# A turn two steps behind its powers, eight buffers for stored exponentials, and a product with one temporary less, in a fused state-space and gated-layer kernel

## The chip, the cores and the metric

One core of one Trainium2 chip. The metric is device microseconds of one execution. Most executions of a kernel agree within 0.3%, so each experiment has five rounds against the kernel before on the same chip (the main comparison has more), and every ratio a 95% interval.

TensorE does the matmuls (PE in the profile, PEld for its weight loads), VectorE is DVE, ScalarE is ACT, GpSimd is POOL, and SyncE (SP) issues most DMAs.

## The reference

Forward and backward of a sum of two branches over a layer-normed input `xn` of 2048 x 576 in bf16: a gated layer (576 to 4608 and back), and a diagonal state-space convolution with 128 states a channel.

```python
K = einsum("dn,dnl,dn->dl", C, exp(dt * A * l), dt * B).real     # kernel rows, 576 x 2048
y = irfft(rfft(K, 2L) * rfft(u, 2L))[:L] + u * Dskip             # convolution
out = x + y(xn) + (relu(xn @ W_gate) * (xn @ W_up)) @ W_down
# asked for: out, and the gradients of all inputs but one
```

## The kernel before

The kernel is written as two Python generators that a driver interleaves. One emits the gated layer (TensorE's main load: lines 235, 261, 288, 325, 341), the other the convolution. A tile scheduler then decides, at build time, the order of the instructions on each engine, and allots buffers from pools. That order is fixed when the kernel runs. An engine that waits for its next instruction does not take a later one that is ready: below, VectorE stands 5.36 us in front of an exponential, while behind it waits a copy (`ps_s_2070`) whose matmul was done at 131.4 us.

The convolution's second stage handles four channels a step, 144 steps in all:

```python
# driver
g.psum_mm = pool("psum_mm", 5, space=PSUM)     # gated layer
g.psum_s4 = pool("psum_s4", 3, space=PSUM)     # convolution: self.ps() takes one of these
...
# p2: for each group of 32 channels, for each half of 16
    ...  # set-up of 16 channels on VectorE and ScalarE, lines 817 to 842; makes A, B, X, XC
    for dd in range(x0, x0 + SX, DG):                       # four channels a step
        V = uvp.tile(...);  Y = yop.tile(...)               # Y: 3 buffers, V: 1
        v.tensor_tensor(vw(Y), Ap(0), Bp(1), op=ALU.mult)   # line 853  "powers"
        v.tensor_tensor(vw(V), Ap(1), Bp(0), op=ALU.mult)   # line 854
        v.tensor_tensor(Y[:], Y[:], V[:], op=ALU.add)       # line 855
        pend.append((Y, XC, X, ...))
        if len(turned) > 0:
            self.sums(turned.pop(0), uvp)
        if len(pend) > 1:                                   # one step behind
            yield from self.turn(pend.pop(0), ytp, turned)

def turn(...):      # "kernel rows and turned powers"
    psk = self.ps() # 8 matmuls of Y with XC, line 879: kernel rows; a copy to Kst
    pst = self.ps() # 8 transposes of Y, line 889; a copy to YT, on ScalarE mostly
def sums(...):
    psg = self.ps() # 8 matmuls of YT, line 902
    for vi, r0 in enumerate((1, 0)):
        nc.vector.tensor_tensor(pr[:, vi], X[...], psg[...], op=ALU.mult)   # line 906, reads PSUM
    nc.vector.tensor_reduce(...)                                            # line 907
```

Two more places are touched. The stored decay exponentials, 36 tiles of 320 KB, are made early and written to DRAM:

```python
exp_ = self.pool(c, "par_ex", 5)
def ex_step(i):
    ex = exp_.tile(shp, F32, name="exs")
    v.tensor_tensor(ex[:], pw..., self.ev..., op=ALU.mult)      # line 568
    nc.scalar.activation(ex[:], ex[:], ACT.Exp)                 # line 569
    nc.sync.dma_start(self.ex_dram[:, i], ex[:])                # line 570
```

And the complex product of two spectra takes seven VectorE instructions, with temporaries `t` and `w` of two rows each.

## Time and profile before

| | before |
|---|---|
| time, median of the first 6 runs | 1805.5 us (1801.1 to 1808.5) |
| TensorE busy / VectorE busy | 95% / 73% of 1800.3 us |
| TensorE idle in 300 to 1500 us (powers, turns, sums) | about 40 us |

The page of the kernel before opens with the busy time, its share of the span and the number of instructions of each engine:

```profile
span 1800.3 us, 41947 instructions
## 1 busy us (share of the span) xinstructions
PE 1711.7 (95%) x16303; PEld 1185.1 (66%) x16449; DVE 1310.8 (73%) x2867; ACT 1187.4 (66%) x2736; POOL 204.3 (11%) x246
```

TensorE bounds the kernel, so time can be won only from its idle 88.6 us and from stretches at a reduced clock. (146 matmul records are missing in this trace, so a few us of that idle time are not real.)

The view of one tile, here the powers `Y` in the kernel before, lists what idle time of an engine just before an instruction that touches the tile was ended by (us in total, number of waits). TensorE (PE) and its weight loads (PEld) are in it, so that one stall of TensorE is mostly counted twice, and VectorE where it writes `Y`:

```profile
its engine sat idle before it (us, times) until:
  DVE V L906: 25.8, 32
  PE ps_s_4647 L889: 15.0, 1
  issue: 8.4, 9
```

Readers of `Y`, which are the turn's matmuls, wait until VectorE's products in `sums` (line 906, which write `V`) are through. Those products have nothing to do with this `Y`. What they free is a PSUM bank: the turn needs one of three, and the sums of the step before hold one until line 906 has read it. The worst case, as the timeline of TensorE and then of VectorE shows it (start, duration, instruction, count, and in brackets the idle time before it with what ended it):

```profile
574.51 0.35 PE L902 MATMUL ps_s_9294<-dkc,YT 128*128 128x32 bf16 x8
574.72 1.26 PE L288 MATMUL ps_mm<-wf,T 128*128 128x288 bf16 x9
575.81 0.29 PE L633 MATMUL ps_s_9322<-pr_z,IM 128*128 128x288 bf16 x1
575.94 0.35 PE L879 MATMUL ps_s_9325<-XC,Y 128*128 128x16 bf16 x8
578.62 0.62 PE L889 MATMUL ps_s_9335<-ident_bf,Y 128*128 128x128 bf16 x8 [2.33 <-DVE V L906]
579.08 2.15 PE L288 MATMUL ps_mm<-wf,T 128*128 128x288 bf16 x9
```

```profile
574.56 0.69 DVE L855 TENSOR_TENSOR Y<-Y,V 128x1024 bf16<-128x1024 bf16 x1
575.16 0.69 DVE L834 TENSOR_TENSOR X<-W,ex 128x512 f32<-128x512 f32 x1
575.88 0.69 DVE L841 TENSOR_TENSOR W<-pw,X 128x512 f32<-128x512 f32 x1
576.49 0.68 DVE L840 TENSOR_TENSOR xa<-pw,X 128x512 f32<-128x512 f32 x1
577.21 0.69 DVE L842 TENSOR_TENSOR XC<-xa,W 128x512 bf16<-128x512 f32 x1
577.82 0.74 DVE L906 TENSOR_TENSOR V<-X,ps_s_9294 128x256 f32<-128x256 f32 x2
```

The sums' matmuls are done at 574.9. Their bank, `ps_s_9294`, is read only at 577.8, because a power and four instructions of the next channels' set-up stand in front on VectorE. Two more banks have gone out meanwhile (9322, 9325), so the transposes (9335) get the first one back and wait 2.33 us. Nine matmuls of line 288 then take 2.15 us where nine took 1.26 before: the trace has the granted clock at 0.50 for 3.41 us from 579.29 us. The Trainium skill ("TensorE: Matmul & The Clock Gate", Part 1) describes a gate that halves TensorE's clock after an idle window.

The other reading that the prediction rests on is about the exponentials. VectorE waits for a free buffer, and a PSUM copy stands behind the waiting instruction (timeline of VectorE, then of TensorE, kernel before):

```profile
123.81 1.55 DVE L568 TENSOR_TENSOR exs<-pw,ev 128x640 f32<-128x640 f32 x2
127.08 0.46 DVE L61 CAST fA_1905<-ps_s_1933 128x288 bf16<-128x288 f32 x1 [1.72 <-PE ps_s_1933 L609]
127.58 0.46 DVE L61 CAST fA_1937<-ps_s_1941 128x288 bf16<-128x288 f32 x1
133.40 0.83 DVE L568 TENSOR_TENSOR exs<-pw,ev 128x640 f32<-128x640 f32 x1 [5.36 <-DMA ex_dram<-exs]
134.14 0.60 DVE L61 CAST obd<-ps_mm 128x432 bf16<-128x432 f32 x1
134.65 0.45 DVE L61 CAST fA_2069<-ps_s_2070 128x288 bf16<-128x288 f32 x1
...
```

```profile
135.16 0.28 PE L609 MATMUL ps_s_2099<-sig,Sx 128*128 128x288 bf16 x1 [2.66 <-DVE fA_2069 L61]
135.28 1.85 PE L325 MATMUL ps_mm<-rows,hN 128*128 128x144 bf16 x16
```

The table of stretches for 130 to 140 us (busy us and instructions of each engine, then the granted clock, the DMA share and GB/s) shows the clock at 0.83 and the DMA engines nearly full:

```profile
130.00:140.00 10.00, 7.34 (x74) 6.59 (x73) 3.05 (x7) 5.28 (x14) 0.00 (x0) 0.83 0.99 348
```

### The profile page before, as it was taken

To read this page: it belongs to the slowest core of one execution; us is meant where nothing else is said; L and a number is where in the kernel's file an instruction comes from. 1 tells how busy PE (TensorE), PEld (TensorE's weight loads), DVE (VectorE), ACT (ScalarE), POOL (GpSimd) and SP (SyncE) were. 2 spreads that over 40 slices of the span, in tenths; PEclk is the share of its full clock that TensorE was granted. 3 is DMA by queue.
4 is the path that set the end of the run, shared out by engine and by line. 5 is a ranking of instruction groups with operands and counts; after the bars stand their busy time and mean duration, and the time that the engine had idled before them with its cause. 6 is when DMAs were issued, how large, how long until landed. Compare 5 with 4: busy or idle time off the path is not lost. (4 is left out here: it accounts for less than half of the span.)

```text
span 1800.3 us, 41947 instructions
## 1 busy us (share of the span) xinstructions
PE 1711.7 (95%) x16303; PEld 1185.1 (66%) x16449; DVE 1310.8 (73%) x2867; ACT 1187.4 (66%) x2736; POOL 204.3 (11%) x246
## 2 busy tenths in 40 slices
PE   7989999999999999999999999999999998999998
PEld 4665557667566666766756766766676675576776
DVE  7575885677888788668777889889888863872551
ACT  5875874696577578568468657748847745864651
POOL 0200011012022012012102101101101100110000
PEclk9999999999999999999999999999999999999999
DMA  8798999678567566766857856756666578994873
GB/s 294 265 331 298 327 248 284 193 188 248 162 138 202 179 177 148 233 182 149 230 152 187 228 168 157 211 168 157 173 179 151 109 213 261 251 289 154 269 241 100
DMA packets 239004, 373.30 MB, mean 207 GB/s; under 512 B 49490, under 2 KB 153428, under 8 KB 237268
## 3 DMA queue, kind: packets, MB, share of 16 engines
q1 hardware_dynamic: 212836, 304.09, 51.6%
q0 software_dynamic: 24384, 51.92, 18.5%
q10 hardware_dynamic: 1584, 14.60, 2.3%
q8 instruction: 129, 2.11, 0.5%
q14 instruction: 71, 0.58, 0.1%
HBM read 233.10 MB, written 137.43 MB: 206 GB/s over the span
## 5 line engine op out<-in xcount | busy, mean ns | idle before, releaser
L288 PE MATMUL ps_mm<-wf,T 128*128 128x288 bf16 x3456 | 484.0, 288 | 8.1 <-DVE T L247 2.5
L288 PEld LDWEIGHTS <-T 128*128 128x128 bf16 x3456 | 324.7, 98 | 95.2 <-issue 11.3
L67 ACT CAST osx<-ps_mm 128x288 bf16<-128x288 f32 x682 | 260.6, 431 | 56.2 <-PE ps_mm L288 53.7
L301 POOL DMA_DIRECT2D acc_dram<-osx x160 | 137.9, 862 | 1050.2 <-ACT osx L67 640.5
L341 PEld LDWEIGHTS <-rows 128*128 128x128 bf16 x1536 | 145.9, 98 | 94.8 <-issue 1.8
L245 DVE SCALAR_TENSOR_TENSOR rg<-rg,ps_mm 128x512 bf16<-128x512 bf16 x144 | 98.6, 684 | 119.1 <-PE ps_mm L235 90.3
L261 PEld LDWEIGHTS <-T 128*128 128x128 bf16 x1728 | 126.9, 98 | 87.9 <-DVE T L247 7.1
L235 PE MATMUL ps_mm<-xT,wd_151 128*128 128x512 bf16 x711 | 178.9, 379 | 0.6 <-issue 0.2
L235 PE MATMUL ps_mm<-gT,wd_152 128*128 128x512 bf16 x694 | 174.7, 379 | 1.5 <-ACT dgN L67 0.6
L235 PE MATMUL ps_mm<-xT,wd_150 128*128 128x512 bf16 x595 | 164.5, 379 | 10.7 <-ACT xT L149 1.6
L261 PE MATMUL ps_mm<-ident_bf,T 128*128 128x128 bf16 x1728 | 157.1, 220 | 7.9 <-DVE T L247 4.3
L325 PE MATMUL ps_mm<-rows,hN 128*128 128x144 bf16 x2304 | 159.1, 227 | 0.0
L325 PEld LDWEIGHTS <-hN 128*128 128x128 bf16 x2304 | 148.5, 98 | 7.6 <-issue 4.9
L67 ACT CAST obw<-ps_mm 128x384 bf16<-128x384 f32 x103 | 49.2, 478 | 140.6 <-PE ps_mm L341 105.8
L341 PE MATMUL ps_mm<-dgN,rows 128*128 128x384 bf16 x768 | 136.1, 326 | 0.7 <-DMA rows<-xs_dram_141 0.7
L341 PE MATMUL ps_mm<-duN,rows 128*128 128x384 bf16 x768 | 136.3, 326 | 0.0
L244 ACT ACTIVATE rg<-ps_mm 128x512 bf16<-128x512 f32 x144 | 87.0, 604 | 54.3 <-PE ps_mm L235 53.0
L67 ACT CAST dhb<-ps_mm 128x512 bf16<-128x512 f32 x141 | 83.8, 594 | 56.2 <-PE ps_mm L235 54.0
L252 DVE TENSOR_TENSOR T<-dhb,rg 128x1024 bf16<-128x1024 bf16 x141 | 99.0, 702 | 26.8 <-ACT dhb L67 26.6
L235 PEld LDWEIGHTS <-wd_150 128*128 128x128 bf16 x720 | 66.2, 97 | 64.1 <-issue 5.2
L235 PEld LDWEIGHTS <-wd_151 128*128 128x128 bf16 x720 | 65.0, 98 | 60.1 <-issue 2.1
L235 PEld LDWEIGHTS <-wd_152 128*128 128x128 bf16 x705 | 63.3, 98 | 58.4 <-DMA gT<-in_gT_dram 1.5
(2504 smaller groups left out, 3050.2 us busy)
## 6 DMA issues: line engine op xcount, KB each, us to landing
acc_dram<-osx POOLq DMA_DIRECT2D x176, 288.0 KB, 5.1
gT<-in_gT_dram SPq DMA_DIRECT2D x48, 640.0 KB, 6.3
xT<-xT_dram SPq DMA_DIRECT2D x44, 640.0 KB, 6.0
rows<-in_gq_dram SPq DMA_DIRECT2D x48, 576.0 KB, 4.1
wf<-in_Wf_dram ACTq DMA_DIRECT2D x11, 1296.0 KB, 8.5
ex_dram<-exs SPq DMA_DIRECT2D x36, 320.0 KB, 4.5
ex<-ex_dram SPq DMA_DIRECT2D x36, 320.0 KB, 3.9
out_dram<-obw SPq DMA_DIRECT2D x96, 96.0 KB, 2.5
```

Source lines behind the costliest of these rows:

```text
L67: self.nc.scalar.copy(out, in_)
L235: nc.tensor.matmul(ps[:], lhsT=w[:, k, fs], rhs=rhs[:, k, :], start=(k == 0), stop=(k == NK - 1))
L244: nc.scalar.activation(rg, ps_g[:], ACT.Relu)
L245: nc.vector.scalar_tensor_tensor(upm, rg, 0.0, ps_u[:], op0=ALU.is_gt, op1=ALU.mult)
L252: nc.vector.tensor_tensor(T[:, 1:3], dhb.unsqueeze(1).to_broadcast([P, 2, JS * P]), ru[:], op=ALU.mult)
L261: nc.tensor.transpose(out=pt[:, j, :], in_=src[:, j * P:(j + 1) * P], identity=g.ident_bf[:])
L288: nc.tensor.matmul(ps[:, cs], lhsT=lt, rhs=rh, start=(i == 0), stop=(i == len(mms) - 1))
L301: nc.gpsimd.dma_start(g.acc_dram[:, t, :, :], o[:], accum_op=ALU.add)
L325: nc.tensor.matmul(ps[:, ft * 144:(ft + 1) * 144], lhsT=self.hN[:, st, ft * P:(ft + 1) * P], rhs=gq[:, st, :], start=(st == 0), stop=(st = ...
L341: nc.tensor.matmul(ps[:, :Fc], lhsT=xs[:, st, 0:P], rhs=src[:, st, :], start=(st == 0), stop=(st == ST - 1))
```

## The change

The intent: give each `Y` a step more before TensorE needs it; stop VectorE from waiting for exponentials' stores; and pay for the extra buffers with a product that needs a row less of temporaries.

```diff
-            exp_ = self.pool(c, "par_ex", 5)
+            exp_ = self.pool(c, "par_ex", 8)
@@ product
-        w = wpool.tile([P, 2, DH], BF16, name="pr_w")
+        w = wpool.tile([P, DH], BF16, name="pr_w")
         v.tensor_tensor(t[:], A, B, op=ALU.mult)
-        for i in range(2):
-            v.tensor_tensor(w[:, i, :], A[:, i, :], B[:, 1 - i, :], op=ALU.mult)
+        v.tensor_tensor(w[:], A[:, 0, :], B[:, 1, :], op=ALU.mult)
 ...  # re and im, im now from t[:, 0] and w
         re(0, top)
+        re(1, low)
+        v.tensor_tensor(t[:, 0, :], A[:, 1, :], B[:, 0, :], op=ALU.mult)
         im(0, top)
         im(1, low)
-        re(1, low)
@@ p2_pools
-            ... ("k_yo", 3), ...
+            ... ("k_yo", 4), ...
@@ p2
-                    if len(pend) > 1:
+                    if len(pend) > 2:
                         yield from self.turn(pend.pop(0), ytp, turned)
```

More of the change, by code (lines that the diff above doesn't have):

```diff
@@ L644, in product @@
         v.tensor_tensor(t[:], A, B, op=ALU.mult)
-        for i in range(2):
-            v.tensor_tensor(w[:, i, :], A[:, i, :], B[:, 1 - i, :], op=ALU.mult)
+        v.tensor_tensor(w[:], A[:, 0, :], B[:, 1, :], op=ALU.mult)
         top, low = slice(0, 64), slice(64, P)
         re = lambda i, r: v.tensor_tensor(Z[0:64, i, :], t[r, 0, :], t[r, 1, :], op=ALU.add if conj else ALU.subtract)
-        im = lambda i, r: v.tensor_tensor(Z[64:P, i, :], w[r, 1, :], w[r, 0, :], op=ALU.subtract if conj else ALU.add)
+        im = lambda i, r: v.tensor_tensor(Z[64:P, i, :], t[r, 0, :], w[r, :], op=ALU.subtract if conj else ALU.add)
         re(0, top)
+        re(1, low)
+        v.tensor_tensor(t[:, 0, :], A[:, 1, :], B[:, 0, :], op=ALU.mult)
         im(0, top)
         im(1, low)
-        re(1, low)
         g.bal.add(d=2.0)
@@ L780, in p2_pools @@
         return (lv,) + tuple(self.pool(c, n, bufs) for n, bufs in (
-            ("k_par", 1), ("k_dr", 1), ("k_dk", 2), ("k_ex", 2), ("k_x", 1), ("k_xo", 2), ("k_uv", 1), ("k_yo", 3), ("k_yt", 2)))
+            ("k_par", 1), ("k_dr", 1), ("k_dk", 2), ("k_ex", 2), ("k_x", 1), ("k_xo", 2), ("k_uv", 1), ("k_yo", 4), ("k_yt", 2)))
     def p2(self, hf, pools, pw):
```

## The prediction

> **What bounds the kernel now.** The page of the kernel before has TensorE busy 1711.7 of 1800.3 us (95%), VectorE 1310.8 (73%), ScalarE 1187.4 (66%). The same matmuls run after the change, so only TensorE's 88.6 us of idle time, and time at a reduced clock, can be won. The table by stretches of 60 us puts about 40 us of that idle time into 300 to 1500 us, where the kernel powers, turns and sums run. There the list of TensorE's waits names VectorE's products in `sums` most: 10.7 us in 14 waits, all of the transposes of `turn`. They wait for a PSUM buffer (three, shared with the convolution), not for Y. A wait for Y itself (line 855) does not appear.
>
> **What the change does.**
> 1. Turn two steps behind. TensorE's work is the same; Y gets one step more (144 steps in 1205 us, 8.4 us) to be ready, for a fourth buffer. Since TensorE hardly waits for Y, and since the transposes wait for the PSUM reader that still stands behind a newer Y on VectorE, I expect 0 to 3 us directly. The opposite wait (VectorE for the sums' matmuls, 82 us in 48 waits) stays, because the lag from turn to sums stays. The instruction orders agree: between turn and sums TensorE streams 12,400 other columns on average before, 12,600 after.
> 2. Product. Seven VectorE instructions of the same shapes (0.46 + 2 x 0.31 + 4 x 0.32 us) in another order; 576 bytes a partition less. It pays for memory: 0 us.
> 3. Eight buffers for the exponentials. In the kernel before VectorE waits 13.6 us, 6 times, for a buffer's store to land (stores land in a median of 4.5 us, at most 8.9, while the DMA share is near 1.0). One of these, 5.4 us from 128.0 to 133.4 us, holds back a PSUM copy, and TensorE stands 2.66 us. Behind it 16 matmuls of line 325 take 1.85 us, twice, against about 1.1 us elsewhere; the granted clock of 130 to 140 us is 0.83. The Trainium skill ("TensorE: Matmul & The Clock Gate", Part 1) says that an idle TensorE falls to half clock and takes about 3.4 us of work to come back; this trace agrees. So this stall costs 2.7 + 1.7 = about 4.4 us. With eight buffers it should go. Against that, the order puts a sixth exponential ahead of two PSUM copies near 104 us, where TensorE already waits: 0.7 us longer.
>
> **Sum.** -3.7 (exponentials), -1 (turn), 0 (product), and a reshuffle of the scheduled order over the whole middle I can't size. From 1805.5 us: **1800 us**, range 1790 to 1810. Chances: faster by over 2% 0.01, within 2% 0.98, slower by over 2% 0.01.
>
> **What would show it.** Right: VectorE's waits for the exponentials' stores fall below 3 us; no TensorE stall near 128 to 135 us, clock 1.00 there; TensorE idle between 300 and 1500 us within 6 us of 40; the transposes' waits for `sums` still there; the product's busy time unchanged. Wrong for step 1: those transposes' waits vanish, or VectorE's 82 us fall by half.
>
> **What would make it wrong.** The exponentials, no longer held back, crowd copies on VectorE and ScalarE, opening another stall over 3 us that halves the clock (now 0.74 at 100 to 110 us); or the new order moves one of the half-clock stalls (570, 270, 1520 us), each worth 3 to 5 us, in or out.

## The result, and the profile after

The changed kernel took 1796.35 us (median of 10 runs, 1790.93 to 1798.13) against 1803.78 us for the kernel before (20 runs). The ratio is 0.9951, 95% interval 0.9938 to 0.9965. Ratios here and below are the mean time of one kernel's runs over that of the other's of the same rounds, so not quite the ratio of the medians quoted.

The page of the changed kernel has the same TensorE work in a shorter span:

```profile
span 1790.0 us, 41927 instructions
## 1 busy us (share of the span) xinstructions
PE 1711.3 (96%) x16306; PEld 1185.2 (66%) x16449; DVE 1318.1 (74%) x2867; ACT 1188.5 (66%) x2736; POOL 204.5 (11%) x246
```

So 10 us of idle time went. The time of the same matmul in both traces tells where: at the end of the second chunk of the gated layer (337 us) the kernels are within 0.5 us of each other, at the end of the tenth (1490 us) the changed one is 6.2 us ahead, at the eleventh (1636 us) 10.3 us, and it stays there. Nothing was won where the exponentials are made: at 298 us, before the first turn, the changed kernel is 1.7 us behind. On the way the lead is not steady (6.6 us at 600 us, 2.2 at 1014). And the last 4.1 us come after the last turn (1470 us), so they are no saved waits of turns. Part of them is a clock stretch: TensorE waits for a DMA before line 624 in both kernels, 2.99 us until 1524 us before and 2.85 us until 1518 us after, and only before is the clock halved behind it, for 3.41 us, which costs 1.7 us.

The view of `Y` in the changed kernel:

```profile
its engine sat idle before it (us, times) until:
  DVE V L906: 8.4, 16
  issue: 4.4, 6
  ACT fC_10464 L67: 2.2, 1
```

The waits for line 906 have fallen from 25.8 to 8.4 us, those of the matmuls alone from 11.6 to 3.3. The exponentials, in the timelines of VectorE and TensorE of the changed kernel:

```profile
124.89 3.02 DVE L568 TENSOR_TENSOR exs<-pw,ev 128x640 f32<-128x640 f32 x4
127.82 0.45 DVE L61 CAST fA_1905<-ps_s_1933 128x288 bf16<-128x288 f32 x1
128.28 0.46 DVE L61 CAST fA_1937<-ps_s_1941 128x288 bf16<-128x288 f32 x1
134.16 0.82 DVE L568 TENSOR_TENSOR exs<-pw,ev 128x640 f32<-128x640 f32 x1 [5.42 <-DMA ex_dram<-exs]
134.90 0.60 DVE L61 CAST obd<-ps_mm 128x432 bf16<-128x432 f32 x1
135.42 0.45 DVE L61 CAST fA_2069<-ps_s_2070 128x288 bf16<-128x288 f32 x1
...
```

```profile
135.92 0.28 PE L609 MATMUL ps_s_2099<-sig,Sx 128*128 128x288 bf16 x1 [2.69 <-DVE fA_2069 L61]
```

```profile
130.00:140.00 10.00, 7.31 (x75) 6.41 (x73) 2.71 (x6) 7.05 (x17) 0.00 (x0) 0.86 0.99 338
```

The same wait, the same stall, the same loss of clock (3.41 us at half clock in both; after, the last part of it lies behind 140 us). In the kernel before the instruction that waits at 128 us is the 14th exponential, and it waits for the buffer of the 9th, whose store lands at 133.3. In the changed kernel it is the 17th, and it waits for the buffer of the same 9th, which lands at 134.1. The scheduler has put three more exponentials in front of the same copies and then run into the same store. The total of such waits is 15.4 us in 6 waits, against 13.6 in 6.

So the total came out inside the predicted range, while of the two steps that carry the sum the larger did not happen and the smaller gained several times what was said. The experiments are about that.

### The profile page after: what moved, and what is told of

It is laid out like the page before. It is cut to its first block, busy times and chain, and to the rows that moved or that the text cites. A ratio compares the mean times of both kernels' runs of the same rounds, so it can differ in the third digit from the quotient of the medians.

```text
span 1790.0 us, 41927 instructions
## 1 busy us (share of the span) xinstructions
PE 1711.3 (96%) x16306; PEld 1185.2 (66%) x16449; DVE 1318.1 (74%) x2867; ACT 1188.5 (66%) x2736; POOL 204.5 (11%) x246
## 4 chain that ended last, share of the span: by engine, by line
PE 64%; DVE 21%; ACT 6%; DMA 5%; issue 3%; SPq 0%; POOL 0%; ACTq 0%; DVEq 0%; POOLq 0%
PE ps_mm L288 17%; PE ps_mm L235 15%; PE ps_mm L341 11%; PE ps_mm L325 7%; PE ps_mm L261 3%; DVE V L906 2%; DVE T L252 2%; DVE Sm L907 2%; DVE V L854 2%; DVE Y L855 2%; DVE Y L853 1%; DVE rg L245 1%; PE ps_mm L358 1%; DMA gT<-in_gT_dram 1%; DVE X L834 1%
```

## The experiments

Three theories. **A**: the gain comes from the turn's lag. **B**, the prediction's: it comes from the exponentials' buffers. **C**: any change of the interleaving moves the time by a few us, and the change was lucky. All runs had correct results and five rounds.

Two columns of the table below were worked out from each run's profile. "Idle at turn and sums" is TensorE's idle time in 300 to 1480 us just before the rows (line 879), the transposes (889) and the sums' matmuls (902). "In front" adds up, over the 144 steps, the time from the end of the sums' matmuls to the start of the VectorE product that reads them, which is how long a PSUM bank lies full and unread; sorted by what VectorE did in it, that is set-up, powers, the gated layer's work and other. Where time "lost to a reduced clock" is given, it is the stretch times one minus its mean granted clock. All three come from one profile a run.

| run | edit | ratio to before (95%) | idle at turn and sums, us | in front, us |
|---|---|---|---|---|
| (before) | | 1 | 20.3 | 129 |
| (changed) | all | 0.9951 (0.9938 to 0.9965) | 8.7 | 96 |
| lag_alone | lag | 0.9958 (0.9941 to 0.9974) | 5.1 | 97 |
| exp_alone | 8 exponentials | 0.9975 (0.9956 to 0.9995) | 20.8 | 128 |
| product_alone | product | 1.0018 (0.9999 to 1.0036) | 19.8 | 121 |
| without_lag | all but lag | 1.0011 (0.9994 to 1.0028) | 20.1 | 118 |
| exp_other_queue | stores on another queue | 1.0058 (1.0038 to 1.0078) | 20.2 | 129 |
| sums_first | priority | 0.9995 (0.9976 to 1.0014) | 18.7 | 108 |
| pace_091 | pace | 1.0036 (1.0019 to 1.0054) | 19.6 | 127 |
| pace_089 | pace | 1.0022 (1.0002 to 1.0042) | 9.4 | 130 |
| psum_4_4 | PSUM 4 + 4 | 0.9923 (0.9905 to 0.9942) | 3.2 | 128 |
| psum_4_4_lag | PSUM 4 + 4, lag | 0.9963 (0.9941 to 0.9984) | 2.4 | 95 |
| lag_and_exp | lag, 8 exponentials | 0.9970 (0.9953 to 0.9987) | 5.0 | 97 |
| lag_three | all, lag of three | 1.0027 (1.0009 to 1.0045) | 4.6 | 76 |

### One part at a time

**lag_alone**, in the kernel before:

```diff
-                    if len(pend) > 1:
+                    if len(pend) > 2:
```

> The kernel before with the turn two steps behind and nothing else (three Y buffers). Theory A, the gain comes from the turn's lag: 0.995 to 0.997 of before, and TensorE's idle time before the transposes of the turn falls from 11 us to under 6. Theory B, the prediction's, the gain comes from the eight exponentials' buffers: 0.999 to 1.000. Theory C, any change of the schedule moves the time by a few us by chance: 0.996 to 1.004, with no tie to these waits.

Measured: 1797.07 us against 1805.55, 0.9958; idle before the transposes 2.7 us. As A said, in waits and in time. (Of the 6.3 us between the two profiles, though, 2.8 are there at 298 us, before the first turn, where the lag can't have saved a wait; 3.8 come between 298 and 1490 us.) The fourth buffer of `Y` isn't needed for it.

**exp_alone**:

```diff
-            exp_ = self.pool(c, "par_ex", 5)
+            exp_ = self.pool(c, "par_ex", 8)
```

> The kernel before with eight buffers for the exponentials and nothing else. Theory A: 0.999 to 1.001, and the stall of TensorE between 128 and 136 us stays, as it does in the changed kernel. Theory B: 0.997 to 0.998, stall gone. Theory C: 0.996 to 1.004.

Measured: 1799.81 us, 0.9975. The time is what B asked for, but its reason is absent: VectorE stands 5.3 us until 133.1 us in front of the 17th exponential, TensorE 2.6 us behind it, and the clock of 130 to 140 us is 0.83. In the profile 1.6 of the 3.6 us of difference to before arise between 483 and 583 us, where the order of instructions on TensorE and VectorE is that of before; one half-clock stretch fewer (1.7 us) fell there. What the 0.25% is stays open; `lag_and_exp` below asks whether it adds to the lag.

**product_alone**: the new product in the kernel before, nothing else.

> The kernel before with the reordered product and nothing else. Theories A and B: 0.999 to 1.001, the same instructions in another order. Theory C: 0.996 to 1.004, since the schedule moves around it.

Measured: 1807.38 us, 1.0018, with an interval that just reaches 1. Its profile is 1.8 us behind that of before at 1014 us and 7.7 us behind at 1368 us, a stretch in which products and turns run together. It is no gain by itself.

**without_lag**: the changed kernel with

```diff
-                    if len(pend) > 2:
+                    if len(pend) > 1:
```

> The changed kernel with the turn one step behind again; product, fourth Y buffer and eight exponentials' buffers stay. Theory A: 0.999 to 1.001 of before, idle time before the turn's transposes back at 9 us or more. Theory B: 0.996 to 0.998. Theory C: anything from 0.996 to 1.004.

Measured: 1807.54 us, 1.0011. Without the lag nothing of the gain is left, and the idle time at the transposes is back at 11.7 us. B, as the prediction argued it, is out: this kernel has the eight buffers.

### Why eight buffers did not help

**exp_other_queue**, in the kernel before:

```diff
-                nc.sync.dma_start(self.ex_dram[:, i], ex[:])
+                nc.scalar.dma_start(self.ex_dram[:, i], ex[:])
```

> The kernel before, five buffers, with the exponentials' stores issued from ScalarE's queue instead of SyncE's. If the buffers were full because stores wait in SyncE's queue behind others (the tenth is issued 19 us after its exponential was ready), VectorE's waits for the stores fall from 13.6 us to under 4, the 5 us wait at 128 us and TensorE's stall behind it go: 0.997 to 0.999 of before. If the stores are slow in the DMA engines themselves, or the schedule packs more exponentials in front of the same copies, the waits stay over 8 us and the time is 0.999 to 1.001.

Measured: 1814.59 us, 1.0058, a miss of the first reading. The waits for stores rose to 25.0 us in 13 waits. The stores land in a median of 5.3 us against 4.5 on SyncE's queue. One part of the first reading did come: TensorE has no idle time between 130 and 140 us, and the clock there is 1.00. It did not pay, since the run is 9.3 us behind by 346 us all the same; TensorE waits 7.3 us for VectorE before line 288 there, and the clock of 95 to 300 us loses 13.7 us against 6.8. So it wasn't the queue alone. That the stores themselves are slow while the DMA engines are this full, and that the exponentials are made as fast as buffers come free, fits the second reading, but is not shown: this run also moved the schedule, and it doesn't separate the two further.

### Is it chance?

**pace_091** and **pace_089** change one constant, `PACE = 0.9`, which sets how far the convolution is let ahead of the gated layer.

> The kernel before with the pace of the convolution's work against the gated layer's at 0.91 instead of 0.90: a shift of the interleaving by about 1% that has no purpose. Size of chance: if any reshuffle of the order moves the time by as much as the lag did, this one or the next shows a difference of 0.3% or more either way; if the lag's gain is its own, both stay within 0.998 to 1.002.

> The same with 0.89 instead of 0.90. Within 0.998 to 1.002 if reshuffles as such cost or gain nothing; 0.3% or more either way if chance is as large as the lag's gain.

Measured: 1811.44 us (1.0036) and 1806.91 us (1.0022). Both are slower, one by more than 0.3%. So a purposeless reshuffle costs as much as the lag gains, and C has to be taken seriously: a single result of 0.4% in this kernel does not explain itself by its sign. What chance does not give is the pattern of the table. The four kernels with the lag on five and three banks have 4.6 to 8.7 us of idle time at turn and sums, and 76 to 97 us in front; the seven others on five and three banks (leaving out the kernel before) have 9.4 to 20.8 and 108 to 130. That pattern is one of waits and not of time: `pace_089`, with 9.4 us at turn and sums, is 0.22% slower than before, and `lag_three`, with 4.6, is 0.27% slower.

### What the lag works through

**sums_first**, in the kernel before:

```diff
-        for vi, r0 in enumerate((1, 0)):
-            nc.vector.tensor_tensor(pr[:, vi], ...)
+        with g.tc.high_priority():
+            for vi, r0 in enumerate((1, 0)):
+                nc.vector.tensor_tensor(pr[:, vi], ...)
```

> The kernel before, turn one step behind, with high scheduling priority for the two VectorE products in the sums that read PSUM. If TensorE's transposes wait because these products stand late in VectorE's order (PSUM theory), idle time before the transposes falls from 11 us to under 6 and the time is 0.996 to 0.998 of before, as the lag alone gave (0.9958). If the lag's gain comes from Y being ready earlier, or is chance, no such fall, 0.999 to 1.001 (chance: 0.997 to 1.003).

Measured: 1803.82 us, 0.9995; idle before the transposes 10.0 us. The edit did not do what it was meant to. Of the 129 us in front, set-up and powers make 82 before and 80 here; only other small work moved away. Why the scheduler left them there was not looked into (it may not reckon the sums' products ready before the set-up). This run decides nothing.

**psum_4_4** takes the wait away itself. In the kernel before:

```diff
-    g.psum_mm = pool("psum_mm", 5, space=PSUM)
-    g.psum_s4 = pool("psum_s4", 3, space=PSUM)
+    g.psum_mm = pool("psum_mm", 4, space=PSUM)
+    g.psum_s4 = pool("psum_s4", 4, space=PSUM)
```

> The kernel before, turn one step behind, with the eight PSUM banks shared four and four instead of five (gated layer) and three (convolution). If TensorE waits before the rows and transposes of the turn (18.6 us together in 300 to 1500 us) because all three banks of the convolution are in use, that idle time falls under 8 us although Y and the lag are as before, and the gated layer may lose as much or more with one bank less: 0.995 to 1.010 of before, so the wait decides this and not the time. If it waits for Y, the idle time stays at 15 us or more.

Measured: 1786.90 us (1786.55 to 1792.05) against 1803.01, 0.9923. The view of `Y` in this run:

```profile
its engine sat idle before it (us, times) until:
  PE ps_s L889: 17.6, 2
  issue: 3.0, 6
  ACT fC L67: 1.8, 3
  PE ps_s L962: 1.0, 1
```

Line 906 is gone from it. Idle time before rows and transposes is 1.8 us, although banks lie unread as long as before (128 us in front) and `Y` is made as early (at least 3.1 us ahead of its turn in both kernels). The wait was for the bank and not for `Y`. (The 17.6 us are VectorE's, waiting for a free `Y` buffer; they were in the kernel before too.) The whole idle time of TensorE in 300 to 1480 us falls from 39.1 to 23.5 us. (101 matmul records of the kernel before are missing in that stretch and none here. Its idle time before line 235 is 5.6 us, against 0.2 in `sums_first` and `exp_other_queue`, which miss none either: so by estimate 5.4 of the 39.1 us are not real, and the fall is about 10 us. The time of the same matmuls puts the gain between 298 and 1490 us at 11.1 us, of 15.7 in all; as in the changed kernel, some 4 us come after the last turn.) And the gated layer, one bank poorer, pays little: idle time before line 288 goes from 5.1 to 10.4 us.

The Trainium skill ("Perfetto Trace Analysis", Identifying Performance Opportunities) says that the same gap repeated on the engine that should be full can mean too little SBUF or PSUM for the next tile. This trace agrees, with 11.6 us in 16 waits of the turn's matmuls for line 906 before and none there after the fourth bank.

**psum_4_4_lag** adds the lag to that.

> The same split of the banks with the turn two steps behind, nothing else. If the lag works through the waits for a PSUM bank, little is left for it: 0.998 to 1.002 of the run with four and four banks. If it works in some other way, it gains the same 0.3 to 0.5% again.

Measured: 1797.39 us, 0.9963 of before, which is 0.9963 / 0.9923 = 1.0040 of `psum_4_4`. On three banks the lag gained 0.42%; on four, where the turn waits for no bank, it gains nothing and loses 0.4%. The loss lies outside the expected 0.998 to 1.002 and is about the size of a pace change. Its idle time is elsewhere: 15.7 us before line 288, against 10.4, and 6.8 us lost to a reduced clock in 300 to 1480 us against none.

### Do the parts add up, and does more lag bring more?

**lag_and_exp**: the two edits of `lag_alone` and `exp_alone` together.

> Lag (three Y buffers) and eight exponentials' buffers, with the old product: the changed kernel without the product's new order and without the fourth Y buffer. If the parts add up (lag 0.9958, exponentials 0.9975): 0.992 to 0.995 of before, faster than the changed kernel. If the exponentials' part was chance: 0.995 to 0.997. If product and fourth buffer are needed for the gain: 0.997 or more.

Measured: 1796.73 us, 0.9970. The sum of the parts would be 0.9933, which lies outside the interval. It lies within the noise of `lag_alone` (0.9958) and not far from the changed kernel (0.9951). So the exponentials' buffers add nothing to the lag. Read the other way, the lag adds nothing to the buffers: 0.9975 without it and 0.9970 with it, although the idle time at turn and sums falls from 20.8 to 5.0 us.

The lag was thus added in four places. On three banks the waits fall each time, while the time between 298 and 1490 us (by the same matmuls, one profile each) falls by very different amounts; on four banks there are hardly any waits to save:

| lag added to | idle at turn and sums, us | time of 298 to 1490 us | ratio to before |
|---|---|---|---|
| before | 20.3 to 5.1 | -3.8 us | 1 to 0.9958 |
| exp_alone | 20.8 to 5.0 | -1.5 us | 0.9975 to 0.9970 |
| without_lag (gives the changed kernel) | 20.1 to 8.7 | -14.9 us | 1.0011 to 0.9951 |
| psum_4_4 | 3.2 to 2.4 | +14.1 us | 0.9923 to 0.9963 |

**lag_three**: the changed kernel with `len(pend) > 3`.

> The changed kernel with the turn three steps behind instead of two, four Y buffers. If the lag gains by what stands in front of the sums' products on VectorE (129 us before, 96 after), a further step brings at most a third of the first one: 0.992 to 0.996 of before, VectorE's work in front of them 80 to 96 us. With Y's buffers all in use VectorE may wait for TensorE instead: 0.996 to 1.000. If the gain was chance: anywhere from 0.994 to 1.004.

Measured: 1809.05 us, 1.0027, a miss. The mechanism goes on, 76 us in front and 4.6 us idle at turn and sums, but the time does not follow: idle time before line 288 is 11.8 us (5.1 before, 6.8 in the changed kernel), before the convolution's other matmuls (lines 609, 624, 633) 13.1 us (2.6 and 6.5), and 6.8 us are lost to a reduced clock in 300 to 1480 us (1.7 in both). The waits at the turn are turned into others.

## Why the prediction was right or wrong

- **The total: right.** 1800 us, range 1790 to 1810, was predicted; 1796.35 was measured. The saving was 7.4 us by medians where 5.5 were forecast. It was right by two errors that offset each other, which is luck; and the range was wide enough to hold the kernel before as well (1805.5), so lying inside it says little.
- **Step 3, the exponentials, -3.7 us: wrong.** This is the step that failed. The failed words are "With eight buffers it should go". The stall at 128 to 135 us stayed, with 2.69 us of TensorE against 2.66, the clock of the stretch at 0.86 against 0.83, and waits of 15.4 us in place of "below 3". The prediction counted which store the 14th exponential would wait for with eight buffers, and left the schedule as it was. The scheduler filled the new buffers with three more exponentials before it came to the same store. The order of instructions of the changed kernel was at hand and showed it: more exponentials in a row ahead of the same copies, four where there had been two.
- **Step 1, the lag, -1 us: mis-sized.** It measured 0.42%, 7.6 us of 1805.55, in `lag_alone`. "A wait for Y itself (line 855) does not appear" was right: in the kernel before every `Y` was ready at least 3.1 us ahead of its turn. "They wait for a PSUM buffer" was right, and `psum_4_4` shows it. The failed step is the inference from there: that the reader "still stands behind a newer Y" and so waits as long. By the order it does: the sums' products of a step stand behind the powers two steps newer before, three steps newer after. But TensorE too comes a step later, so what counts is how much of that VectorE work is still undone then. That fell from 129 to 96 us: powers from 33 to 18, set-up (lines 817 to 842) from 49 to 40, the rest from 47 to 38. VectorE also waits for the sums' matmuls more often, 58 times against 48, which fits that it is there first more often. The prediction itself named "those transposes' waits vanish" as what would prove step 1 wrong, and they fell from 10.7 us in 14 waits to 3.2 in 7.
- **"VectorE for the sums' matmuls, 82 us" stays: right**, 86.7 us.
- **Step 2, the product, 0 us: right as to its instructions**, which take the 0.46 and 0.31 us each in the changed kernel that they took before; not proved as to the kernel: 1.0018, at the edge of its interval.
- **"TensorE idle between 300 and 1500 us within 6 us of 40": wrong**, it fell by 7.2 us in 300 to 1480 us (39.1 to 31.9).
- **The "reshuffle of the scheduled order"** that it couldn't size: two changes of pace made 0.2 and 0.4%, both slower. What it feared, that the new order moves a half-clock stall in or out, happened: the half-clock stretches at 579 and 1525 us of the kernel before are gone in the profile after, and one at 646 us is new.

What is shown: without the lag nothing of the changed kernel's gain is left (`without_lag`), and the lag alone gives about as much in the kernel before (`lag_alone`); it shortens the waits at the turn on three banks wherever it is added; these waits are for a PSUM bank (`psum_4_4`); with a bank more it has nothing to gain. What is not shown: that the saved waits are the gain in time. With the same waits saved, the lag was worth 0.60% on `without_lag`, 0.42% on before and 0.05% on `exp_alone`, and a purposeless reshuffle costs as much as it gains, so theory C stands for the size of the gain, though not for the waits. What is only argued: that the scheduled order lets VectorE run a step further ahead and so work off a set-up before the sums arrive.

The version that beats both is the kernel before with four and four banks: 1786.90 us, 0.9923 of before, about twice the largest effect of a pace change.

## What to carry to other kernels

When a busy engine waits for a reader of a shared PSUM ring, first try one bank more in that ring: a rearrangement that makes the reader prompter treats the same wait indirectly, and here gained nothing once the bank was there. Don't count a shortened wait as time saved: here 11 to 16 us of waits less were worth 1.5 to 15 us. A deeper buffer ring under a scheduler that runs ahead may be filled at once and end at the same slow store; look at which item waits for which, in the new order and not in the old one. And before explaining a difference of half a per cent, run a change or two without a purpose to see what the order alone is worth.

## What the Trainium skill lacked or had wrong

- "TensorE: Matmul & The Clock Gate", Why this matters for your kernels, asks for no idle gaps over about 3 us. Shorter ones were enough here: after 2.33 us of idle time at 578.6 us, nine matmuls of 288 columns took 2.15 us in place of 1.26. It was not regular: TensorE's stalls of 2.66 and 2.69 us near 135 us left clocks of 0.83 and 0.86 in their 10 us, and in `lag_alone` that stretch, with 2.15 us idle, stayed at 1.00. The free-running window of Part 1 fits this, and the traces show it: in the kernel before half-clock stretches start at 104.84, 135.56, 272.09, 579.29 and 1524.78 us, which are 9, 40, 90 and 277 times 3.413 us apart. What counted was the idle time inside one such window, not the length of the stall. In the 14 traces, from 95 us to 6 us before the end, 75 windows at full clock were followed by half clock, and they had at least 1.44 us of idle time (all but three at least 1.8); the 6778 that were not had at most 2.02 us. So a window about half idle was enough, where Part 1 speaks of an idle one. The 2.33 us stall of the kernel before lay in one window. The same 2.33 us stall in `exp_alone`, until 577.3 us, was cut into 1.20 and 1.14 us by a boundary, and the clock stayed at 1.00. So where a stall falls on this grid is part of the scatter, 1.7 us a stretch.
- "PSUM — Partial Sum Buffer" tells of the eight banks, but not what their division between two streams of work is worth. Here 5 + 3 against 4 + 4 was 0.77% of the whole kernel.
- No page says that the order fixed at build time is itself a source of scatter: two changes of one pacing constant by about 1% moved the time by 0.36% and 0.22%.
